# A float32 attention and gated-unit kernel: token sums, weight splits, a query-and-key unit and two steps' loads at other places in the order

## The chip, the cores and the metric

One core of a Trainium2 chip runs the whole program in one launch. The metric is device time in microseconds. The run without a profile was timed three times; the execution that the profile shows is one more run with a time of its own.

## What is computed

The reference, cut to what matters (S=2048 tokens, D=512, H=32 heads of 16, F=1792, float32):

```python
g = sigmoid((x * gate_w).sum(-1, keepdims=True))
q, k, v = split(x @ wqkv)                      # 32 heads of 16
a = softmax(q @ k.T / 4) @ v                   # per head
a = concat(a) @ wo
h = sigmoid(x @ w_gate) * (x @ w_up)
b = h @ w_down
return g * a + (1 - g) * b
```

## The kernel before

Every float32 product is made of three TensorE matmuls on a value's high part and its low part (`h`, `l`): high times high, high times low, low times high. `split` rounds a value to its high part and subtracts it for the low part.

**Startup.** The tokens come as four column blocks `x0` to `x3` of 512 and are split into `xt0` to `xt3` (ring tag "xt", four buffers). Queries and keys of the first head pairs are made at once and sent through DRAM (`q_d`, `k_d`) into the score operands `QS`, `KS`. Then a loop over t = 2, 4, ..., 14 makes the values `v` of two token tiles each, the "token sums". Each pair of sums runs in two halves of the matmul array: first the rows that are LOW for one and UP for the other, then the reverse. Both halves write one PSUM bank, so between them stands a `turn`: an empty instruction in POOL's own queue that waits for the last matmul of the first half, and for which the second half waits (L213 to L218). Since it is in POOL's queue, it also comes after whatever was put there before it. In between, `first_max` makes the first scores and VectorE their row maxima.

POOL's other work is queued in the list `later`, and `work(n)` takes n jobs from it. Generators put jobs there: `filling` (`next(fill)`) the splits of the next query and key weights (`q1`, `k1`) and later the mixtures of weights; `mixing` (`next(mix)`) pieces of token mixtures `xm`, each a load, an addition where it has one, a rounding and a subtraction. In a token sum the last lines are

```python
if g == LOW:
    turn(*two)
    next(mix)
    work(5)
```

**The periods.** 256 periods k (n = 2k) follow, each by a word list (STEADY; for the last eight LAST): score matmuls and exponentials (t), the next scores' row maxima (m), halves of dense work (d). At a period's end come `turn(run)`, `work(...)` and `values(k)`, the product of probabilities and v (L846). The dense work is a list of units: two direct query-key products, three mixed query-key units, 14 gate and up units of the first two token blocks (each made of seven half products of mixtures `xm` and of weight mixtures `mh`, `ml`), then the same for the other blocks, with the query-key unit `qk3_1` at their head (L461 to L463). Last come two down products made ahead, for the token tiles 13 and 4 (SECOND, AHEAD): `hidden_ahead` reads gate and up rows `ha` back from DRAM, makes hidden values on ScalarE and POOL and stores them (`h_d`); `load_ahead` reads them into `hh`.

The row maxima of a group of 16 score tiles are closed by `close_max`: halves on POOL (`mxs`), a transpose on VectorE (`mt`, L345), then `send` (L351): four small DMAs from `mt` into the score operand `qs`. Two groups are sent in four periods; each is needed when, two periods on, its first scores begin.

**The queues.** Nearly all DMAs are issued by SyncE (SP), in order. The instruction order of TensorE, ScalarE, VectorE and POOL is the order of the code; that of SyncE is chosen by the scheduler. SyncE's DMAs signal on eight semaphores in turn, so that one waits for the one eight before it. `take(n)` issues n loads of the list `parts` (late mixtures, `hh`).

**The last loop** goes over 28 steps `chunks` (a token block and two rows of F): `hidden_load` reads gate and up rows (`gul`, 2 x 512 KB), `hidden` and `hidden_split` make hidden values, L1074 multiplies by w_down. Step 0 and 1 are loaded in the periods, 2 to 4 behind them, and each step loads the one five ahead.

Of the kernel before, what the change touches and what calls it, by code (L numbers as in the profile page):

```python
# [26 lines left out]
P = 128  # L27
KT = D // P
# [27 lines left out]
def gated_mix(ctx, tc, x, xc, xmix, wqk, w_qk, wv, wo, w_gu, w_down, gate_w, out):  # L56
# [177 lines left out]
    xes = ExitStack()  # L234
# [3 lines left out]


# [6 lines left out]
    def split_x(c, raw):  # L246
        xt.append(xp.tile([P, 2, KT, 512], F32R, name=f"xt{c}", tag="xt", bufs=4))
        for k in range(KT):
            split(xt[c][:, 1, k, :], xt[c][:, 0, k, :], raw[:, k, :], act, dve)
# [106 lines left out]
    def mixing(pair, T=(), here=0):  # L356
# [27 lines left out]
        for n, (j, b) in enumerate(pieces):  # L384
# [5 lines left out]
            if j < here and b == 0:  # L390
                T[j] = xp.tile([P, 2, KT, 512], F32R, name=f"xm{pair}_{j}", tag="xt", bufs=4)
# [6 lines left out]
    def mixed(pair, j):  # L398
        t = xp.tile([P, 2, KT, 512], F32R, name=f"xm{pair}_{j}", tag="xt", bufs=4)
# [62 lines left out]
    units += [queries_keys(D // P - 1, 1)]  # L462
    units += [gate_up(1, fp, a) for fp in range(NF // 2) for a in range(2)]  # L463

# [54 lines left out]
    def load_ahead(t, lo, hi):  # L519
        if t not in held:  # L520
            held[t] = xp.tile([P, 2, KT, 512], F32R, name=f"hh{t}", tag="xt", bufs=4).rearrange(
# [19 lines left out]
    def filling():  # L541
# [16 lines left out]
        for j, (n, cp) in enumerate(DIRECT):  # L558
            settle([raw for raw, _, _ in coming])
            ws, nxt = nxt, []  # L560
            for c in range(2):
                for i, w in enumerate(ws):
# [6 lines left out]
                    for _ in range(2 if runs < 3 else 1):  # L569
# [16 lines left out]
        for u, (name, _, store) in enumerate(units):  # L586
# [3 lines left out]
            for q, (j, g) in enumerate(order):  # L590
# [7 lines left out]
                leave(e, run.o)  # L598
# [14 lines left out]
                take(1 if u == both - 1 and late_t and q < 4 else 2)  # L613
# [52 lines left out]
    sp.dma_start(gwb, gate_w.unsqueeze(0).to_broadcast([P, D]))  # L666
    next(fill)
# [41 lines left out]
    for t in range(2, NS, 2):  # L709
        two = [Sum(bankv(), tokens(t + a)) for a in range(2)]  # L710
        for g in (LOW, UP):
# [16 lines left out]
            if g == LOW:  # L728
                turn(*two)
                next(mix)  # L730
                work(5)
# [10 lines left out]
    def hidden_load(c, f):  # L742
# [5 lines left out]
        for a in range(2):  # L748
            sp.dma_start(gu[:, a], gu_d[a, f:f + 2, :, c * 512:(c + 1) * 512].rearrange("f p s -> p f s"))
        return gu  # L750

# [165 lines left out]
    ahead_h = []  # L917
    for k in range(NPER):
# [33 lines left out]
        if n in (456, 458, 460, 462, 464, 466):  # L952
            if n % 4 == 0:
                part_ahead = hidden_ahead((n - 456) // 4, SECOND)
            next(part_ahead)
        if n in (304, 308, 312, 316):
            ahead_h.append(hidden_ahead((n - 304) // 4))
            next(ahead_h[-1])
        if n in (308, 312, 316, 320):
            next(ahead_h[(n - 308) // 4])  # L960
# [14 lines left out]
        if k == EARLY - 2:  # L975
            loaded.extend(hidden_load(*chunks[m]) for m in range(2))
        if NPER - TAIL + 2 <= k < NPER - TAIL + 6:
# [19 lines left out]
    loaded.extend(hidden_load(*chunks[m]) for m in range(2, 5))  # L997
# [19 lines left out]
    def heads_split(u, ot, rb):  # L1017
        oh = lp.tile([P, KT, 256], F32R, name=f"oh{u}", tag="oh", bufs=2)
        ol = lp.tile([P, KT, 256], F32R, name=f"ol{u}", tag="ol", bufs=2)
# [127 lines left out]
```

## Time and profile before

| | us |
|---|---|
| runs without a profile | 1667.78, 1663.26, 1664.01 (median 1664.01) |
| the profiled execution | 1670.4 |
| its span, first to last instruction | 1668.2 |
| VectorE, ScalarE, POOL busy in it | 1429.0, 1341.6, 1156.9 |

The page of the profile cuts the span into 40 equal slices of 41.7 us. A digit is the busy share in tenths (9 is 90% or more); PEclk is the clock that TensorE was granted, in tenths of full speed, and GB/s is what the DMA engines moved:

```profile
PE   9799999999999999999999999999999999999999
POOL 1457698978878877767668798777677789864111
PEclk9899999999999999999999999999999999999999
DMA  9535754344453444232664253434343347458871
```

TensorE's row and its clock each have one 7 or 8, in the second slice (41.7 to 83.4 us), which is the token sums' place. The DMA row is full in the first slice (the tokens' loads) and near its end (the last loop's loads).

### The profile page before, as it was taken

How to read it: one execution, taken by the hardware profiler on the slowest of the kernel's cores; microseconds unless marked ns; L12 is line 12 of the kernel's file. 1: busy time of each engine (PE TensorE's matmuls, PEld its weight loads, DVE VectorE, ACT ScalarE, POOL GpSimd, SP SyncE). 2: the span in 40 equal slices, each digit the busy share in tenths (PEclk: the TensorE clock that was granted, in tenths of full speed). 3: DMA queues.
4: the chain of work that ended last, by engine and by line, in shares of the span. 5: the costliest groups of instructions: out<-in, count | busy, mean ns of one | idle time of the engine just before them, and what ended most of it. 6: DMA issues, size and time to landing. Idle time of an engine off the chain costs nothing.

```text
span 1668.2 us, 44281 instructions
## 1 busy us (share of the span) xinstructions
PE 1646.7 (99%) x16830; PEld 1168.4 (70%) x16830; DVE 1429.0 (86%) x2460; ACT 1341.6 (80%) x2944; POOL 1156.9 (69%) x1334
## 2 busy tenths in 40 slices
PE   9799999999999999999999999999999999999999
PEld 7676666667667666666666666666767766667887
DVE  6689999999999999999989999999999999648645
ACT  4168898898889889889879999999999998875322
POOL 1457698978878877767668798777677789864111
PEclk9899999999999999999999999999999999999999
DMA  9535754344453444232664253434343347458871
GB/s 260 153 113 170 212 165 109 116 128 147 133 161 114 138 128 134 84 110 71 183 185 127 82 144 125 102 96 105 95 106 106 90 128 253 131 187 283 267 257 51
DMA packets 136148, 239.87 MB, mean 144 GB/s; under 512 B 19904, under 2 KB 43456, under 8 KB 132928
## 3 DMA queue, kind: packets, MB, share of 16 engines
q1 hardware_dynamic: 135648, 236.52, 47.8%
q8 instruction: 133, 2.18, 0.6%
q14 instruction: 79, 0.65, 0.1%
q10 hardware_dynamic: 288, 0.52, 0.1%
HBM read 161.22 MB, written 75.24 MB: 142 GB/s over the span
## 4 chain that ended last, share of the span: by engine, by line
PE 94%; DMA 3%; DVE 1%; SPq 1%; POOL 1%; ACT 0%; issue 0%; DVEq 0%; ACTq 0%; POOLq 0%
PE dn L178 30%; PE sm L846 16%; PE st L846 12%; PE sm L321 6%; PE sm L700 5%; PE st L700 4%; PE st L321 4%; PE sm L1074 4%; PE st L145 3%; PE dn L158 3%; PE dn L1074 2%; PE st L1074 2%; PE st L158 1%; PE dn L204 1%; PE sm L145 1%; DMA r<-in_w_gu_dram 1%
## 5 line engine op out<-in xcount | busy, mean ns | idle before, releaser
L323 DVE TENSOR_REDUCE stat<-sm 128x1 f32<-128x512 f32 x1199 | 764.2, 682 | 84.5 <-PE st L700 47.1
L702 ACT ACTIVATE p<-sm 128x512 f32<-128x512 f32 (+1 forms) x1308 | 666.6, 598 | 11.4 <-PE sm L700 10.9
L323 DVE TENSOR_REDUCE stat<-st 128x1 f32<-128x512 f32 x849 | 550.4, 683 | 48.1 <-PE sm L700 44.3
L702 ACT ACTIVATE p<-st 128x512 f32<-128x512 f32 (+2 forms) x988 | 519.9, 598 | 0.7
L178 PE MATMUL dn<-xm,mh 64*128 64x512 f32 x1568 | 485.1, 389 | 0.0
L321 PE MATMUL sm<-ks,qs 48*128 48x512 f32 x1199 | 477.2, 420 | 0.5 <-DVE stat L323 0.3
L700 PE MATMUL sm<-qs,ks 64*128 64x512 f32 (+1 forms) x1308 | 471.8, 383 | 4.5 <-DMA qs<-mt 4.5
L700 PE MATMUL st<-qs,ks 64*128 64x512 f32 (+2 forms) x988 | 365.2, 383 | 0.0
L321 PE MATMUL st<-ks,qs 48*128 48x512 f32 x849 | 357.8, 422 | 0.0
L178 PE MATMUL dn<-xm,ml 64*128 64x512 f32 x784 | 304.3, 388 | 0.0
L178 PEld LDWEIGHTS dn<-xm,mh 64*128 64x128 f32 x1568 | 289.9, 185 | 16.1
L846 PE MATMUL sm<-p,v 128*17 128x256 f32 x4704 | 282.5, 381 | 0.0
L700 PEld LDWEIGHTS sm<-qs,ks 64*128 64x128 f32 x1308 | 234.6, 187 | 67.4 <-DVE stat L323 57.5
L321 PEld LDWEIGHTS sm<-ks,qs 48*128 48x128 f32 x1199 | 211.4, 185 | 35.1 <-ACT p L702 26.7
L846 PEld LDWEIGHTS sm<-p,v 128*17 128x17 f32 x4704 | 123.6, 97 | 131.4 <-ACT p L702 44.7
L700 PEld LDWEIGHTS st<-qs,ks 64*128 64x128 f32 x988 | 179.1, 187 | 48.9 <-DVE stat L323 44.5
L846 PE MATMUL st<-p,v 128*17 128x256 f32 x3488 | 209.4, 381 | 0.1
L470 POOL TENSOR_TENSOR m<-m,m 128x512 f32<-128x512 f32 x140 | 178.1, 1289 | 1.3 <-ACT m L630 1.3
L321 PEld LDWEIGHTS st<-ks,qs 48*128 48x128 f32 x849 | 157.5, 185 | 23.5 <-ACT p L702 19.9
L872 POOL TENSOR_TENSOR sum<-sum,part 128x256 f32<-128x256 f32 x192 | 142.0, 739 | 42.2 <-ACT part L851 28.2
L846 PEld LDWEIGHTS st<-p,v 128*17 128x17 f32 x3488 | 91.7, 97 | 97.1 <-ACT p L702 33.2
L178 PEld LDWEIGHTS dn<-xm,ml 64*128 64x128 f32 x784 | 144.4, 184 | 10.6
(381 smaller groups left out, 2473.7 us busy)
## 6 DMA issues: line engine op xcount, KB each, us to landing
r<-in_w_gu_dram SPq DMA_DIRECT2D x112, 256.0 KB
gul<-gu_d SPq DMA_DIRECT2D x56, 512.0 KB
gu_d<-m SPq DMA_DIRECT2D x84, 256.0 KB
xm<-in_xmix_dram SPq DMA_DIRECT2D x24, 512.0 KB
xm_d<-xm SPq DMA_DIRECT2D x24, 512.0 KB
xm<-xm_d SPq DMA_DIRECT2D x24, 512.0 KB
qs<-q_d SPq DMA_DIRECT2D x90, 128.0 KB
ks<-k_d SPq DMA_DIRECT2D x90, 128.0 KB
```

The source lines that it names most:

```text
L145: pe.matmul(o, a, b, start=(i == 0), stop=(i == len(ops) - 1))
L158: mm = pe.matmul(self.o, a[rows], b[rows], start=(self.n == 0), stop=(self.n == 2 * len(self.ops) - 1))
L178: pe.matmul(self.o, a, b, start=(self.n == 0), stop=(self.n == len(self.ops) - 1))
L204: mm = pe.matmul(o, a[rows], b[rows], start=(alone not in self.begun), stop=last)
L321: pe.matmul(t, qs[r:r + KM, qt * P:(qt + 1) * P], ks[r:r + KM, g * 512:(g + 1) * 512], start=True, stop=True)
L323: dve.tensor_reduce(stat[part][:, qt % 4, g:g + 1], t, axis=AX.X, op=ALU.max)
L470: pool.tensor_tensor(o, x, y, op)
L700: pe.matmul(o, ks[r:r + KR, (kt + a) * P:(kt + a + 1) * P], qs[r:r + KR, c * 512 + lo:c * 512 + hi], start=True, stop=True)
L702: exps.append(act.activation(pt[:, a, lo:hi], o, AF.Exp, scale=DH ** -0.5))
L846: pe.matmul(o[r:r + VW, :], v[:, 4 * k % 16 + a, h * VW:(h + 1) * VW], pts[b][:, a, 256 * i:256 * i + 256], start=(a == 0), stop=(a == 3))
L872: added.append(pool.tensor_tensor(s, s, e, ALU.add))
L1074: pe.matmul(down[t], a, b, start=(f == begin and m == 0), stop=(f == NF - 2 and m == 5))
```

## The change

- **Token sums.** `next(mix)` is called once ahead of `next(fill)`, so the first mixture's load is the list's first job and the four weight splits come after it. In the loop over t, `next(mix)` and `work(n)` follow small tables: 1 job at t=2, 4 at t=6, 10 and 12, 12 at t=14, none at 4 and 8. The direct units call `next(mix)` twice after units 1, 3 and 5, where it was after 1 and 2.
- **Buffers.** `tokens_tile` gives the tiles of token block or mixture 3 a buffer of their own (`xq`) and leaves three to the ring of the others. After the last use of mixture 3 its buffer becomes `apart`, which holds the gate and up rows of steps 2 and 3. Behind the periods the steps 4 and 5 are loaded, and each step loads the one six ahead. `oh`, `ol` of the heads move to the side that `xq` frees at step 3.
- **Unit `qk3_1`** stands behind two gate and up units of the second half, no longer ahead of them.
- **Hidden values ahead** for tile 4 are made from n=282 to 310, one part of them at a time (before 304 to 320, overlapping); those for tile 13 from n=448 to 466 (before 456 to 466). The loads of `hh` in the last unit each wait for that unit step's eviction (`left`). In the first unit `take` issues one load, not two, at a time.

```diff
--- before.py
+++ after.py
@@ -231,11 +231,17 @@
     va = keep.tile([P, NS * VROW], F32, name="v", tag="va")
     v = va.rearrange("p (t c) -> p t c", t=NS)
     QS, KS = zip(*[(big(f"qs{b}", F32R), big(f"ks{b}", F32R)) for b in range(2)])
-    xes = ExitStack()
+    xes, xqs = ExitStack(), ExitStack()
+    xq = xqs.enter_context(tc.tile_pool(name="xq", bufs=1, side="right"))
     xp = xes.enter_context(tc.tile_pool(name="xp", bufs=1))
     xt = []
     gwb = xp.tile([P, D], F32, name="gwb")
 
+
+    def tokens_tile(j, name, dt=F32R):
+        if j < 3:
+            return xp.tile([P, 2, KT, 512], dt, name=name, tag="xt", bufs=3)
+        return xq.tile([P, 2, KT, 512], dt, name=name, tag="xt")
 
     def load_x(c):
         raw = mid(f"x{c}")
@@ -244,7 +250,7 @@
         return raw
 
     def split_x(c, raw):
-        xt.append(xp.tile([P, 2, KT, 512], F32R, name=f"xt{c}", tag="xt", bufs=4))
+        xt.append(tokens_tile(c, f"xt{c}"))
         for k in range(KT):
             split(xt[c][:, 1, k, :], xt[c][:, 0, k, :], raw[:, k, :], act, dve)
 
@@ -388,7 +394,7 @@
                 if sign:
                     later.append(lambda n=n, r=rows, op=ALU.add if sign == "+" else ALU.subtract: add(loaded[n], r, op))
             if j < here and b == 0:
-                T[j] = xp.tile([P, 2, KT, 512], F32R, name=f"xm{pair}_{j}", tag="xt", bufs=4)
+                T[j] = tokens_tile(j, f"xm{pair}_{j}")
             later.append(lambda n=n, j=j, b=b: high(loaded[n], j, b))
             later.append(lambda n=n, j=j, b=b: low(loaded[n], j, b))
             if n + 1 < len(pieces):
@@ -396,7 +402,7 @@
         yield
 
     def mixed(pair, j):
-        t = xp.tile([P, 2, KT, 512], F32R, name=f"xm{pair}_{j}", tag="xt", bufs=4)
+        t = tokens_tile(j, f"xm{pair}_{j}")
         for b in range(4):
             parts.append(lambda b=b: sp.dma_start(t[:, :, b, :].bitcast(F32), xm_d[pair, j, :, :, b, :]))
         return t
@@ -459,8 +465,8 @@
     units = [queries_keys(n, 0) for n in range(1, D // P)]
     units += [gate_up(0, fp, a) for fp in range(NF // 2) for a in range(2)]
     both = len(units)
-    units += [queries_keys(D // P - 1, 1)]
     units += [gate_up(1, fp, a) for fp in range(NF // 2) for a in range(2)]
+    units.insert(both + 2, queries_keys(D // P - 1, 1))
 
     def combine(store):
         e = {}
@@ -518,7 +524,7 @@
 
     def load_ahead(t, lo, hi):
         if t not in held:
-            held[t] = xp.tile([P, 2, KT, 512], F32R, name=f"hh{t}", tag="xt", bufs=4).rearrange(
+            held[t] = tokens_tile(0, f"hh{t}").rearrange(
                 "p i k s -> p i (k s)")[:, :, :NF * P].rearrange("p i (f s) -> p i f s", s=P)
         for i in range(2):
             parts.append(lambda i=i: sp.dma_start(held[t][:, i, lo:hi].bitcast(F32), h_d[t][:, i, lo:hi]))
@@ -566,7 +572,7 @@
                     e = keep.tile([P, 512], F32R, name=f"qk{n}_{cp}_{c}_{i}", tag="er", bufs=6)
                     left = leave(e.bitcast(F32), run.o)
                     put_qk(e, (q_d, k_d)[i], n, 2 * cp + c)
-                    for _ in range(2 if runs < 3 else 1):
+                    for _ in range(2 if runs in (1, 3, 5) else 1):
                         next(mix, None)
                     if j + 1 < len(DIRECT):
                         if (c, i) == (0, 0):
@@ -595,7 +601,7 @@
                 yield run
                 m = ((2, 1), (4, 3), (7, 6), (5, 5))[j][g]
                 e = keep.tile([P, 512], F32, name=f"m{m}_{name}", tag="er", bufs=6)
-                leave(e, run.o)
+                left = leave(e, run.o)
                 if arrived:
                     arrived.pop(0)()
                 arrived.append(lambda arrive=arrive, m=m, e=e: arrive(m, e))
@@ -610,7 +616,7 @@
                 last = u == len(units) - 1
                 if last and q in AHEADS:
                     load_ahead(*AHEADS[q])
-                take(1 if u == both - 1 and late_t and q < 4 else 2)
+                take(1 if u == 0 or u == both - 1 and late_t and q < 4 else 2, left if last else None)
                 if last and q:
                     weights_ahead()
             flip ^= 1
@@ -664,6 +670,7 @@
         if c % 2:
             list(load_pair(0, slice((c - 1) * 512, (c + 1) * 512)))
     sp.dma_start(gwb, gate_w.unsqueeze(0).to_broadcast([P, D]))
+    next(mix)
     next(fill)
     w_v = [(wv_h[:, k, :], wv_l[:, k, :]) for k in range(KT)]
     bankv = turns([bankd()] + banks)
@@ -727,8 +734,9 @@
                     closed.append([4, turned])
             if g == LOW:
                 turn(*two)
-                next(mix)
-                work(5)
+                for _ in range({4: 1, 10: 1, 12: 1, 14: 2}.get(t, 0)):
+                    next(mix)
+                work({2: 1, 6: 4, 10: 4, 12: 4, 14: 12}.get(t, 0))
         if t < NS - 2:
             for a in range(2):
                 put_v(t + a, two[a].o, act)
@@ -746,8 +754,11 @@
             gu = big(f"gul{c}_{f}")
         gu = gu.rearrange("p (a f s) -> p a f s", a=2, f=2)
         for a in range(2):
-            sp.dma_start(gu[:, a], gu_d[a, f:f + 2, :, c * 512:(c + 1) * 512].rearrange("f p s -> p f s"))
+            hidden_part(gu, a, c, f)
         return gu
+
+    def hidden_part(gu, a, c, f):
+        sp.dma_start(gu[:, a], gu_d[a, f:f + 2, :, c * 512:(c + 1) * 512].rearrange("f p s -> p f s"))
 
     def late_raw(src, r):
         raw = keep.tile([P, 2, D], F32, name=f"late{r}", tag="ev", bufs=2)
@@ -914,7 +925,6 @@
         put_v(NS - 2 + a, two[a].o, engine)
     bank = bankm = place
     stages = [[], []]
-    ahead_h = []
     for k in range(NPER):
         n = 2 * k
         if 320 <= n < 448 and n % 16 == 0:
@@ -949,15 +959,14 @@
         if k >= EARLY - 4:
             for _ in range((1, 2, 2, 2, 2, 2, 1, 1, 2, 2, 2, 1, 1)[k - EARLY + 4] if k < EARLY + 9 else 0):
                 weights_ahead()
-        if n in (456, 458, 460, 462, 464, 466):
-            if n % 4 == 0:
-                part_ahead = hidden_ahead((n - 456) // 4, SECOND)
+        if n in (448, 452, 454, 458, 462, 466):
+            if n in (448, 454, 462):
+                part_ahead = hidden_ahead((n - 448) // 6, SECOND)
             next(part_ahead)
-        if n in (304, 308, 312, 316):
-            ahead_h.append(hidden_ahead((n - 304) // 4))
-            next(ahead_h[-1])
-        if n in (308, 312, 316, 320):
-            next(ahead_h[(n - 308) // 4])
+        if 282 <= n < 314 and n % 4 == 2:
+            if n % 8 == 2:
+                ahead_h = hidden_ahead((n - 282) // 8)
+            next(ahead_h)
         work(run.jobs if isinstance(run, Side) else 5 if k < 16 or EARLY - 4 <= k < NPER - TAIL else 3 if k % 2 else 4)
         urgent.extend(jobs)
         if 320 <= n < 448:
@@ -974,6 +983,11 @@
         values(k)
         if k == EARLY - 2:
             loaded.extend(hidden_load(*chunks[m]) for m in range(2))
+            apart = tokens_tile(3, "apart", F32)
+            loaded.extend(apart[:, m].rearrange("p (a f) s -> p a f s", a=2) for m in range(2))
+        if EARLY <= k < EARLY + 4:
+            m, a = divmod(k - EARLY, 2)
+            hidden_part(loaded[2 + m], a, *chunks[2 + m])
         if NPER - TAIL + 2 <= k < NPER - TAIL + 6:
             early_hidden(*divmod(k - NPER + TAIL - 2, 2))
         if n == NSTEP - 16:
@@ -994,7 +1008,7 @@
 
     xes.close()
     lp = ctx.enter_context(tc.tile_pool(name="lp", bufs=1))
-    loaded.extend(hidden_load(*chunks[m]) for m in range(2, 5))
+    loaded.extend(hidden_load(*chunks[m]) for m in range(4, 6))
     wd_h = lp.tile([P, NF - 6, D], F32R, name="wd_h")
     wd_l = lp.tile([P, NF - 6, D], F32R, name="wd_l")
     weights = keep.tile([P, NS * VROW], F32R, name="weights", tag="va")
...
@@ -1055,6 +1069,9 @@
     at = dict(zip((9, 11, 13, 15, 18, 20, 23, 25), range(8)))
     heads = {}
     for n, (c, f) in enumerate(chunks):
+        if n == 3:
+            xqs.close()
+            lq = ctx.enter_context(tc.tile_pool(name="lq", bufs=1, side="right"))
         if f == 0:
             down = [bankt() if 4 * c + t != AHEAD else None for t in range(4)] if c else six[2:]
         if n == 4:
@@ -1080,8 +1097,8 @@
                 finish(4 * c + t, o, g0)
             if n == t == 0:
                 last_values()
-        if n + 5 < len(chunks):
-            loaded.append(hidden_load(*chunks[n + 5]))
+        if n + 6 < len(chunks):
+            loaded.append(hidden_load(*chunks[n + 6]))
         if n == 9:
             next(denominators(1))
         if n == 20:
```

What moves on the engines is shown at three places. The names: `q1r`, `k1r` are raw weights and `q1h`, `q1l`, `k1h`, `k1l` their parts; `xm_a_b` is piece b of mixture a; `mtP_i_b` are the maxima of head pair P, query block i, head b; `hN_d` and `haN` are hidden values ahead for tile N; `gu_d` holds gate and up rows; `wdNr` are raw rows of w_down.

**POOL in the token sums.** Rows from the end of the weight splits on (`turn`s are no rows here: before, that of t=4 stands right behind `k1l`; now that of t=6 stands ahead of `q1h` and that of t=8 behind `k1l`). Before:

```order
L131 TENSOR_TENSOR k1l_371<-k1r_366,k1h_370 128x512
L367 TENSOR_TENSOR xm0_0_0_441<-xm0_0_0_441 64x512
L371 CAST xm0_0_520<-xm0_0_0_441 128x512
L376 TENSOR_TENSOR xm0_0_520<-xm0_0_0_441,xm0_0_520 128x512
L367 TENSOR_TENSOR xm0_0_1_524<-xm0_0_1_524 64x512
L371 CAST xm0_0_520<-xm0_0_1_524 128x512
L376 TENSOR_TENSOR xm0_0_520<-xm0_0_1_524,xm0_0_520 128x512
L367 TENSOR_TENSOR xm0_0_2_600<-xm0_0_2_600 64x512
L371 CAST xm0_0_520<-xm0_0_2_600 128x512
L376 TENSOR_TENSOR xm0_0_520<-xm0_0_2_600,xm0_0_520 128x512
L108 CAST mxs_112<-mxs_112 128x4
L109 TENSOR_TENSOR mxs_112<-mxs_112 128x4
```

Now:

```order
L131 TENSOR_TENSOR k1l_374<-k1r_369,k1h_373 128x512
L108 CAST mxs_115<-mxs_115 128x4
L109 TENSOR_TENSOR mxs_115<-mxs_115 128x4
L108 CAST mxs_115<-mxs_115 128x4
L109 TENSOR_TENSOR mxs_115<-mxs_115 128x4
L373 TENSOR_TENSOR xm0_0_0_440<-xm0_0_0_440 64x512
L377 CAST xm0_0_519<-xm0_0_0_440 128x512
L382 TENSOR_TENSOR xm0_0_519<-xm0_0_0_440,xm0_0_519 128x512
L373 TENSOR_TENSOR xm0_0_1_758<-xm0_0_1_758 64x512
```

The halves of the first two maxima (128x4) have moved from behind three pieces of mixture 0 to right behind the weight splits.

**SyncE ahead of the send for period 160** (`mt10_0_0`). Before:

```order
L509 DMA h4_d_79<-ha4_0_13535 256x1x512
L451 DMA gu_d_76<-den_100 128x512
L502 DMA ha4_2_13869<-gu_d_76 128x4x128 x2
L351 DMA qs0_103<-mt10_0_1_13771 2x4x32 x4
L874 DMA pv_d_77<-sum9_2_13557 128x256
L451 DMA gu_d_76<-m3_1_0_1_13529 128x512
L451 DMA gu_d_76<-m1_1_0_1_13373 128x512
L419 DMA r2_1_1_1_14206<-in_w_gu_dram 128x512
L419 DMA r3_1_1_1_14372<-in_w_gu_dram 128x512
L509 DMA h4_d_79<-ha4_1_13696 256x1x512
L502 DMA ha4_3_14034<-gu_d_76 128x2x128 x2
L351 DMA qs0_103<-mt10_0_0_13946 2x4x32 x4
```

Now:

```order
L357 DMA qs1_105<-mt9_3_0_13619 2x4x32 x4
L357 DMA qs0_103<-mt10_0_1_13782 2x4x32 x4
L885 DMA pv_d_77<-sum9_2_13568 128x256
L515 DMA h4_d_79<-ha4_3_13628 256x1x256
L835 DMA xn2_14814<-in_x_dram 128x2x512
L281 DMA k_d_74<-qh3_3_13793 128x512
L281 DMA k_d_74<-den_100 128x512
L425 DMA r2_1_1_1_14214<-in_w_gu_dram 128x512
L357 DMA qs0_103<-mt10_0_0_13954 2x4x32 x4
```

The store and load of `ha4` right ahead of the send are gone; one such store stands five rows ahead, with a logit load behind it, and the stores of the keys of `qk3_1` have come in.

**SyncE around the sends for periods 240 and 244** (`mt15_0_0`, `mt15_1_0`). Before:

```order
L524 DMA hh4_20443<-h4_d_79 128x640 x4
L524 DMA hh4_20443<-h4_d_79 128x512 x2
L351 DMA qs1_105<-mt15_0_0_20522 2x4x32 x4
L113 DMA wd8r_20864<-in_w_down_dram 128x512
L113 DMA wd9r_20868<-in_w_down_dram 128x512
L451 DMA gu_d_76<-den_100 128x512
L749 DMA gul0_0_20979<-gu_d_76 128x2x512 x2
L749 DMA gul0_2_20982<-gu_d_76 128x2x512 x2
L351 DMA qs1_105<-mt15_1_1_20690 2x4x32 x4
```

Now, and, in the second piece, the rows up to the send for period 244:

```order
L530 DMA hh4_20447<-h4_d_79 128x640 x2
L530 DMA hh13_20276<-h13_d_80 128x512 x2
L357 DMA qs1_105<-mt15_0_0_20526 2x4x32 x4
L113 DMA wd8r_20867<-in_w_down_dram 128x512
L113 DMA wd9r_20871<-in_w_down_dram 128x512
L530 DMA hh4_20447<-h4_d_79 128x640 x2
L457 DMA gu_d_76<-den_100 128x512
L113 DMA wd10r_20954<-in_w_down_dram 128x512
L761 DMA gul0_0_20982<-gu_d_76 128x2x512 x2
L761 DMA gul0_2_20985<-gu_d_76 128x2x512
L530 DMA hh4_20447<-h4_d_79 128x512 x2
L357 DMA qs1_105<-mt15_1_1_20694 2x4x32 x4
```

```order
L761 DMA gul0_2_20985<-gu_d_76 128x2x512
L761 DMA apart_20988<-gu_d_76 128x2x512 x2
L457 DMA gu_d_76<-m3_1_6_1_20445 128x512
L457 DMA gu_d_76<-m1_1_6_1_20274 128x512
L113 DMA wd11r_20958<-in_w_down_dram 128x512
L761 DMA apart_20988<-gu_d_76 128x2x512 x2
L113 DMA wd4r_21044<-in_w_down_dram 128x512
L357 DMA qs1_105<-mt15_1_0_20861 2x4x32 x4
```

The six loads of `hh4` in one go ahead of the first send have become three pairs, two of them behind it; four loads into `apart` (512 KB each) are new ahead of the second.

More of the change, by code (lines that the diff above doesn't have):

```diff
@@ L1017, in heads_split @@
     def heads_split(u, ot, rb):
-        oh = lp.tile([P, KT, 256], F32R, name=f"oh{u}", tag="oh", bufs=2)
-        ol = lp.tile([P, KT, 256], F32R, name=f"ol{u}", tag="ol", bufs=2)
+        oh = lq.tile([P, KT, 256], F32R, name=f"oh{u}", tag="oh", bufs=2)
+        ol = lq.tile([P, KT, 256], F32R, name=f"ol{u}", tag="ol", bufs=2)
         for j in range(2):
```

## The prediction

> **What bounds the kernel now.** The page comes first: busy time by engine, then the chain that ended last.
>
> ```profile
> PE 1646.7 (99%) x16830; PEld 1168.4 (70%) x16830; DVE 1429.0 (86%) x2460; ACT 1341.6 (80%) x2944; POOL 1156.9 (69%) x1334
> ```
>
> ```profile
> PE 94%; DMA 3%; DVE 1%; SPq 1%; POOL 1%; ACT 0%; issue 0%; DVEq 0%; ACTq 0%; POOLq 0%
> ```
>
> TensorE is busy 99% of the span of 1668.2 us and carries 94% of the chain. The change takes no matmul away, so what it can gain is TensorE's idle time and the time at a reduced clock. The view of TensorE's waits lists nearly all of the first:
>
> ```profile
> PE dn L158 <- POOLq L215: 10.0, 1, 10.0
> PE sm L700 <- DMA qs<-mt: 4.5, 3, 2.7
> PE sm L1074 <- DVE hl L109: 1.4, 1, 1.4
> ```
>
> Five waits, then: one at the start (a turn, L215), three in the periods (row maxima that come late from `send`, L351), one in the last loop. Each is followed to its cause.
>
> **The startup wait.** TensorE's timeline (start, length, engine, line, tiles; in brackets the idle time before it and what ended it):
>
> ```profile
> 44.49 0.50 PE L321 MATMUL sm<-ks,qs 48*128 48x512 f32 x2
> 54.97 0.79 PE L158 MATMUL dn<-wv_h,xt 64*128 64x512 f32 x1 [9.97 <-POOLq L215]
> ...
> 58.87 0.39 PE L158 MATMUL dn<-wv_h,xt 64*128 64x512 f32 x1
> 59.10 0.39 PE L158 MATMUL dn<-wv_h,xt 64*128 64x512 f32 x1
> ```
>
> Pairs of half-array matmuls start 0.23 us apart (58.87, 59.10). Between the lower halves of the token sums t=4 and their upper halves lie 54.97 - 44.49 = 10.48, so 10.25 are lost. From 54.97 to 58.87 the order has nine places (eight pairs of halves and a pair of scores), which take 3.90 instead of 9 x 0.23 = 2.07: another 1.83. The windows view shows the clock of that stretch:
>
> ```profile
> 55.00:59.60 4.60, 4.60 (x26) 3.64 (x28) 1.24 (x2) 0.00 (x0) 4.37 (x4) 0.59 0.29 48
> ```
>
> The last three numbers are the granted clock (0.59), the share of the DMA engines and GB/s. The cause is on POOL's timeline:
>
> ```profile
> 52.36 0.61 POOL L135 CAST q1h<-q1r 128x512 fp32r<-128x512 f32 x1 [43.54 <-DMA q1r<-in_wqk_dram]
> ...
> 54.94 1.27 POOL L131 TENSOR_TENSOR k1l<-k1r,k1h 128x512 fp32r<-128x512 f32 x1
> ...
> 72.72 1.29 POOL L376 TENSOR_TENSOR xm<-xm,xm 128x512 fp32r<-128x512 f32 x1
> 73.97 0.18 POOL L108 CAST mxs<-mxs 128x4 fp32r<-128x4 f32 x1
> ```
>
> `work(5)` at t=2 puts the four splits of q1 and k1 into POOL's queue, the first waits until 52.36 for its weights, and the turn of t=4 stands behind k1l (54.94). In the change t=2 pops only the first mixture's load and the splits come behind the turn of t=6. Turn t=4 then meets an empty queue: **-10.25, and -1.83** for the clock that fell with it. Late next is the turn of t=8, behind k1l, which still ends at 54.94 + 1.27 = 56.21. The sums of t=8 begin at 66.74 now (next part), so 12.1 earlier at 54.7, and their upper half half of 6.9 later, at 58.1: 1.9 us of cover. What the weights land later than that is lost.
>
> **Token sums t=10.** The scores' first call marks where a pair of sums begins (t=8, 10, 12, 14, then the first period); the row apart is VectorE's:
>
> ```profile
> 66.74 0.40 PE L321 MATMUL sm<-ks,qs 48*128 48x512 f32 x2
> 73.64 0.46 PE L321 MATMUL sm<-ks,qs 48*128 48x512 f32 x2
> 82.55 0.49 PE L321 MATMUL sm<-ks,qs 48*128 48x512 f32 x2
> 89.56 0.40 PE L321 MATMUL sm<-ks,qs 48*128 48x512 f32 x2
> ...
> 98.40 0.39 PE L321 MATMUL sm<-ks,qs 48*128 48x512 f32 x1
> ```
>
> ```profile
> 74.47 0.31 DVE L345 STREAM_TRANSPOSE mt<-mxs 128x128 f32<-128x128 f32 x1 [1.88 <-POOL mxs L109]
> ```
>
> t=8 takes 6.90, t=10 **8.91**, t=12 7.01: 1.96 over the mean of its neighbours. VectorE stood 1.88 before the transpose because the maxima's halves (73.97) were queued behind a mixture piece (72.72 and its two neighbours); TensorE then ran out of score banks. In the change the halves stand right behind k1l, ahead of any piece, on an idle POOL. Bounds: all of 1.96 goes, or only 1.0 (the halves still take two small operations and a hop each way). I take **-1.6**, near the full amount, since the piece in front is gone altogether.
>
> The pieces land elsewhere: twelve jobs at t=14 are three pieces, each (1.29 + 0.61 + 1.29, some 3.3 with gaps), 10 us of POOL from about 79.0 (89.56 + 3.4 - 14), ending near 89 or, with the maxima's halves between them, 89.5. The first turn of the periods is queued behind them and needed when the second period begins, 98.40 - 14 + 5.4 = 89.8: nothing in the best case, 3.0 if the last piece's load is a piece (3.3) late. I take **+0.4**, near the lower end, as the queue alone just fits.
>
> **The three late maxima.** SyncE's timeline (its DMA issues) ahead of each, and the transpose that made the data ready, for the two whose queue changes:
>
> ```profile
> 965.67 0.59 SPq L509 DMA_DIRECT2D h_d<-ha  x1
> 968.72 0.89 SPq L502 DMA_DIRECT2D ha<-gu_d  x2
> 969.70 2.67 SPq L351 DMA_DIRECT2D qs<-mt  x4
> ...
> 1399.90 2.76 SPq L524 DMA_DIRECT2D hh<-h_d  x6
> 1402.75 2.65 SPq L351 DMA_DIRECT2D qs<-mt  x4
> ```
>
> ```profile
> 961.68 0.30 DVE L345 STREAM_TRANSPOSE mt<-mxs 128x128 f32<-128x128 f32 x1
> ```
>
> At 961.98 the maxima were ready; the queue held them 7.7 us, first for POOL's hidden-ahead values, then for the loads behind that store. TensorE lost about 0.9, so a send may start some 6.8 late before it costs anything. In the change the hidden-ahead work comes five to eleven periods earlier, one part at a time, so POOL is not behind when this store comes: **-0.9**. The third stands behind six hh loads in one burst; in the change two are taken per unit step, each behind its eviction, and part-ahead starts four periods earlier: **-0.9** (4.5 - 2.7 leaves 1.8 for both). Bounds for the pair: 0 to -1.8.
>
> The first and largest is different:
>
> ```profile
> 850.70 1.23 SPq L401 DMA_DIRECT2D xm<-xm_d  x2
> 851.99 2.57 SPq L419 DMA_DIRECT2D r<-in_w_gu_dram  x4
> 854.66 3.82 SPq L351 DMA_DIRECT2D qs<-mt  x4
> ```
>
> ```profile
> 851.33 1.06 PE L846 MATMUL st<-p,v 128*17 128x256 f32 x16
> 856.76 1.27 PE L846 MATMUL st<-p,v 128*17 128x256 f32 x20
> 867.67 1.92 PE L846 MATMUL sm<-p,v 128*17 128x256 f32 x32
> ```
>
> ```profile
> 861.30:864.60 3.30, 3.23 (x17) 2.78 (x19) 2.05 (x3) 2.16 (x5) 0.04 (x1) 0.50 0.68 235
> ```
>
> The values of a period come every 5.43 (851.33, 856.76), here after 10.91: 5.48 lost, the wait of 2.7 and a half clock (0.50) after it. Ahead of the send stand the late mixtures' loads and the raw rows of one unit. The change replaces a query-and-key unit's raw rows there by a gate-and-up unit's, of the same sizes in the same order; the mixtures' loads stay. So **0**; bound -5.5.
>
> **Tail and the two steps loaded early.** The 1.4 before L1074 belongs to the fifth step, whose eviction waits for rows that come last in a crowded queue. In the change they keep their place, behind five other loads of 512 KB: **0**, bound -1.6 (the wait with its restart). Four such loads more, written for periods 244 to 247, stand in SyncE's order close ahead of the send for period 244, 2.1 MB. What flows there now, in five microseconds each:
>
> ```profile
> 1405.00:1410.00 5.00, 4.12 (x53) 2.42 (x51) 3.76 (x9) 3.64 (x9) 4.92 (x8) 1.00 0.81 267
> 1415.00:1420.00 5.00, 5.00 (x60) 3.39 (x57) 4.72 (x11) 4.04 (x10) 4.84 (x6) 1.00 0.97 359
> ```
>
> Over two periods (10.9 us) they add 193 GB/s to 267, and 460 is 101 above the 359 that were carried: 1.1 MB, or 3.1 us behind. They use an empty buffer and nothing waits for them; a send behind them may. I take **0**, as 3.1 is under the cover of 6.8; bounds 0 and +5.5, the price of the period above. The moved unit's stores and the logit loads have work around them on every engine; a missed place costs a period's tenth at most: 0.
>
> **Sum.** -10.25 - 1.83 - 1.6 + 0.4 - 0.9 - 0.9 = -15.1. Of the profiled execution's own 1670.4 us (span 1668.2) 1655.3 would be left. The runs without a profile have a median of 1664.0 (1663.3 to 1667.8), 6.4 less; the terms are stalls of the program's order and not of the profiler, so I take them off that: **1648.9, say 1649**.
>
> **Rivals.**
> 1. *The stall at period 140 goes as well*, since its cause is lateness of transfers, and a shifted POOL or fewer takes in the first unit may empty the queue. For it: the send needs to gain only some 3 us. Against: rows and order ahead of it are the same. 1649 - 5.5 = 1643.5, with the tail's 1.6 gone 1642.
> 2. *A new late send at period 244*, behind the added loads: +0.9 (like 160) to +5.5 (like 140), so 1650 to 1654.5. For it: 460 GB/s has no room, and the send is right behind. Against: 3.1 of the 6.8 is used.
> 3. *The startup wait only moves to t=8* (the change doesn't do what it says), if the weights of q1 and k1 land over 1.9 later; each further microsecond costs one. Twelve late would give 10.1 back: 1659. Against: their loads keep their place in the queue.
> 4. *Slower*: SyncE's queue falls behind from 240 to 255 for good, because each hh load waits for an eviction and holds all that is behind it, while the added loads fill the transfers. All four lower sends of that stretch would then stall like period 140: 4 x 5.5 = 22, or 1671. It decides where sends start more than 6.8 late four times running; above 20.1 added the kernel is slower by over 0.3%. Now only one of these four is late, by 0.9.
>
> The trace has a wait of 2.7 us followed by a clock of 0.50. The Trainium skill ("TensorE: Matmul & The Clock Gate", What's actually happening) has the gate throttle after at least one idle window of about 3.4 us, free-running, and open again after as much work. By that a wait of 2.7 would cost 2.7 alone, rival 2 would end at 1651.7, and rival 4 would come to 4 x 2.7 - 15.1, still faster. The trace disagrees on the length (2.7 was enough) and agrees on the way back (3.9 us at half speed after the first wait).
>
> **How the numbers follow.** Forecast 0.53 (its own range 1646 to 1652), rival 1 0.22, rival 2 0.17, rival 3 0.05, rival 4 0.03. The range runs from rival 1 with the tail (1642) to rival 2's end with the first turn's bound (1654.5 + 2.6, about 1657); 8 in 100 lie outside. A measurement of this kernel tells 0.3% (5 us) from no change: faster 0.92 (forecast, rivals 1 and 2), same 0.05 (rival 3), slower 0.03.
>
> **What will show it.** The row of L215 at 10 us gone from TensorE's waits; token sums t=4 and t=10 at 6.9 to 7.0 like the others; no clock under 0.9 between 40 and 80; k1l's end at about 56 and the turn of t=8 without idle time. Waits for qs<-mt: one of about 2.7 near 845, and nothing near 959 and 1393; a row near 1414 is rival 2. The forecast is wrong if startup still has a wait over 2 us, or if more than one send is late behind the periods' middle.

## The result, and the profile after

| | us |
|---|---|
| before, without a profile | 1664.13 (median of 6, 1663.26 to 1667.78) |
| changed, without a profile | 1655.76 (median of 6, 1654.81 to 1658.87) |
| ratio | 0.9948, 95% interval 0.9935 to 0.9961 |
| profiled execution, before and changed | 1670.4 and 1655.2 (spans 1668.2 and 1653.0) |

Faster by about 8.4 us, inside the stated range, but 6.8 above the forecast of 1649. The two profiled executions differ by 15.2 us, almost exactly the 15.1 of the forecast's sum. That agreement is an accident, as the sections below show: most of the sum's terms were right, three costs were missing, and the first profile of the kernel before held a stall that is much smaller in every other one.

TensorE's waits in the changed kernel, in the form shown for before (released by, total us, times, longest):

```profile
PE sm L707 <- DMA qs<-mt: 2.9, 2, 1.7
PE st L93 <- DVE warm L89: 1.0, 1, 1.0
PE dn L158 <- POOLq L215: 0.5, 1, 0.5
```

The turn's wait of 10.0 in the startup is gone; the 0.5 belongs to another turn, one of a direct query-key product. The late maxima come to 2.9 in two waits (4.5 in three), and the last loop's 1.4 is gone. Apart from the 1.0 ahead of the warm-up matmuls, none of these waits is where one was before. POOL's timeline of the changed token sums:

```profile
53.40 0.61 POOL L135 CAST q1h<-q1r 128x512 fp32r<-128x512 f32 x1 [44.58 <-DMA q1r<-in_wqk_dram]
...
56.02 1.29 POOL L131 TENSOR_TENSOR k1l<-k1r,k1h 128x512 fp32r<-128x512 f32 x1
61.50 0.19 POOL L108 CAST mxs<-mxs 128x4 fp32r<-128x4 f32 x1 [4.19 <-DVE mxs L341]
...
67.29 1.29 POOL L373 TENSOR_TENSOR xm<-xm 64x512 f32<-64x512 f32 x1 [3.19 <-DMA qs<-mt]
```

The weights still land late (53.40), but no turn waits for them now, and the maxima's halves (61.50) find POOL idle. The calls that mark the starts of t=8, 10 and 12, and of the first period:

```profile
55.59 0.40 PE L327 MATMUL sm<-ks,qs 48*128 48x512 f32 x2
...
62.51 0.45 PE L327 MATMUL sm<-ks,qs 48*128 48x512 f32 x2
...
70.07 0.53 PE L327 MATMUL sm<-ks,qs 48*128 48x512 f32 x2
...
85.96 0.39 PE L327 MATMUL sm<-ks,qs 48*128 48x512 f32 x1
```

The first period starts at 85.96 (98.40 before): 12.4 earlier, though this execution began later by itself. The 16 warm-up matmuls at the very start, the same in both kernels, before and changed:

```profile
1.02 5.26 PE L93 MATMUL st<-warm 128*128 128x512 f32 x16 [1.02 <-DVE warm L89]
```

```profile
1.02 6.25 PE L93 MATMUL st<-warm 128*128 128x512 f32 x16 [1.02 <-DVE warm L89]
```

They end 1.0 us later here, and some 0.8 of it is left at the upper half of t=4 (its first call at 45.32, before at 44.49). So token sums and turn have gained about 13.3 (12.4 and 0.8).

What is new is a late send at period 16. A period's length is taken here from the start of its values to the start of the next period's; undisturbed it is 5.43.

```profile
171.95 0.84 PE L857 MATMUL sm<-p,v 128*17 128x256 f32 x12
...
175.60 0.32 PE L707 MATMUL sm<-qs,ks 64*128 64x192 f32 x1 [1.73 <-DMA qs<-mt]
...
180.61 0.62 PE L857 MATMUL st<-p,v 128*17 128x256 f32 x8
```

```profile
175.00:180.00 5.00, 4.40 (x27) 3.56 (x29) 3.27 (x5) 3.62 (x8) 4.84 (x8) 0.68 0.56 134
```

Period 15's values at 171.95 are followed by the next after 8.66 instead of 5.43: 1.73 of waiting and a clock of 0.68 behind it cost 3.23. SyncE's timeline shows what stands ahead of the send:

```profile
164.89 0.34 SPq L368 DMA_DIRECT2D xm<-in_xmix_dram  x1
165.33 1.25 SPq L407 DMA_DIRECT2D xm<-xm_d  x2
166.66 0.54 SPq L281 DMA_DIRECT2D q_d<-qh  x1
167.30 0.39 SPq L281 DMA_DIRECT2D q_d<-qk  x1
167.78 0.66 SPq L385 DMA_DIRECT2D xm_d<-xm  x1
168.54 3.13 SPq L357 DMA_DIRECT2D qs<-mt  x4
```

and the chain ahead of the wait:

```profile
165.33 5.70 DMA xm<-xm_d
171.05 4.42 DMA qs<-mt
```

One piece of a token mixture is loaded and another stored ahead of the send, with two 512 KB loads of the late mixtures between them; the send's fourth DMA waits for one of those loads (5.70) and lands after 4.42 itself. The send starts 2.0 us into its period (168.54, the period's values at 166.52); in the kernel before, the same send started 0.7 into it. The rows ahead of it were the same there, in the same order, but earlier in their period: the piece's load waits until its buffer's store has landed, and that store now starts 1.0 us later and takes 8.1 to land (6.1 before), so that the load goes out 1.6 us ahead of the values instead of 4.7.

Two smaller ones: a turn of the direct products costs 0.7 at period 9 (period 8 lasts 6.16; a mixture piece stands ahead of the turn in POOL's queue until 135.9), and a send for period 244 costs 1.2, rival 2's place. That send's second DMA goes out at 1410.93, when a load into `apart` that was issued eight DMAs before it, at 1402.23, has landed. Periods 160 and 240 are clean, as forecast.

### The profile page after: what moved, and what is told of

Its sections match the earlier page's. It is cut to its first block, busy times and chain, and to the rows that moved or that the text cites. A ratio compares the mean times of both kernels' runs of the same rounds, so it can differ in the third digit from the quotient of the medians.

```text
span 1653.0 us, 44265 instructions
## 1 busy us (share of the span) xinstructions
PE 1644.4 (99%) x16830; PEld 1168.0 (71%) x16830; DVE 1428.8 (86%) x2460; ACT 1341.1 (81%) x2944; POOL 1158.5 (70%) x1334
## 4 chain that ended last, share of the span: by engine, by line
PE 95%; DMA 2%; POOL 1%; ACT 1%; DVE 0%; issue 0%; SPq 0%; POOLq 0%; ACTq 0%
PE dn L178 31%; PE sm L857 16%; PE st L857 12%; PE sm L327 6%; PE sm L707 5%; PE sm L1091 4%; PE st L707 4%; PE st L327 4%; PE st L145 3%; PE st L1091 2%; PE dn L158 2%; PE dn L1091 2%; PE st L158 1%; PE sm L145 1%; ACT p L709 1%; DMA gu_d<-m 1%
```

## The experiments

Each ratio is to runs of the kernel before that were made beside it, so experiments are compared by their ratios; the brackets hold its 95% interval.

**The kernel before, profiled again** (no edit).

> The kernel before, unchanged, profiled a second time. Question: is the 5.5 us stall of period 140 part of every execution? Theory A (it is one execution's, set off by late transfers): TensorE's waits for qs<-mt have no row near 2.7, the period with values at 856.76 takes about 5.4 like the others, and the span is 1661 to 1663.5. Theory B (it belongs to the program's order, and the change took it away): it is there again with 2 to 3 us of waiting, span 1666 to 1669. By both, the turn's wait of 10 us (L215) and two waits of about 0.9 at periods 160 and 240 are there.

One run, 1665.37, span 1663.1. TensorE's waits:

```profile
PE dn L158 <- POOLq L215: 11.2, 1, 11.2
PE sm L700 <- DMA qs<-mt: 2.0, 2, 1.1
PE st L93 <- DVE warm L89: 1.0, 1, 1.0
PE sm L1074 <- DVE hl L109: 0.7, 1, 0.7
```

No wait near 2.7, and the span is theory A's. Period 139 lasts 6.59 here (10.91 in the first profile), not 5.4; it has one of the two waits that are left, and the other is that of period 160. Period 240 has none, which neither theory had. The start is again a turn of over 10 us. So the 5.5 us of period 140 were one execution's, on top of a send that is close to its limit (in the changed kernel's two profiles that period lasts 5.51 and 6.91). The difference is most of the first profile's 6.4 us over the median.

**The token-sum edits alone**, on before:

```diff
+    next(mix)
     next(fill)
...
-                next(mix)
-                work(5)
+                for _ in range({4: 1, 10: 1, 12: 1, 14: 2}.get(t, 0)):
+                    next(mix)
+                work({2: 1, 6: 4, 10: 4, 12: 4, 14: 12}.get(t, 0))
...
-                    for _ in range(2 if runs < 3 else 1):
+                    for _ in range(2 if runs in (1, 3, 5) else 1):
```

> Before, with only the token-sum edits of the change: one call of the mixture generator ahead of the weight splits, the two tables over t, and the direct units' calls after units 1, 3 and 5. Theory A (the changed kernel's new waits at periods 9 and 16 come from the mixture pieces that these edits move later): startup 13.3 us shorter, the turn's wait of about 0.5 near 135 and a late send near 173 are there, cost 0.7 + 3.2, so 9 to 10 us less than before: about 1654.5; the two waits of 0.9 stay. Theory B (those waits come from the three-buffer ring or from the other edits): neither wait is there, 13.3 less: about 1651.

1653.52, ratio 0.9942 (0.9927 to 0.9957): theory A. The turn's 0.5 is there, period 8 lasts 6.14 and period 15 lasts 8.17, as in the changed kernel:

```profile
PE sm L701 <- DMA qs<-mt: 4.5, 3, 2.7
PE st L93 <- DVE warm L89: 1.0, 1, 1.0
PE dn L158 <- POOLq L215: 0.5, 1, 0.5
```

The 2.7 is now period 16's; 0.9 each stay at 160 and 240. These edits alone bring the whole gain of the change (its ratio of 0.9948 lies in their interval).

**The token-sum edits with one piece more in startup**, on before. The pieces keep the old kernel's pace in the direct units:

```diff
-                next(mix)
-                work(5)
+                for _ in range({4: 1, 10: 2, 12: 1, 14: 2}.get(t, 0)):
+                    next(mix)
+                work({2: 1, 6: 4, 10: 8, 12: 4, 14: 12}.get(t, 0))
```

> Before, with the token-sum edits but two mixture pieces behind the turn of t=10 (one more piece done in startup) and the direct units' calls after units 1 and 2 as before. Theory A (pace of the pieces): the row of 10 us is gone, there is no wait of a turn near 135 and none over 0.5 us for a late send near 173, so about 13 less than before: 1651. Theory B (the two waits come from elsewhere): they stay, and it takes about what the startup edits alone take. Both: the two pieces end by about 74, as the turn of t=12 is needed, so up to 0.5 of waiting there.

1653.44, ratio 0.9938 (0.9923 to 0.9953). No wait at 9 and none at 16, as theory A has it, but the time is that of the startup edits alone, as theory B has it. A turn's wait of 1.0 in the first periods takes part of the gain back: the sixth piece's load comes behind eight small DMAs of a send, and POOL waits 2.64 for it ahead of the turn. Another 1.1 is a wait in the last loop, which nothing here explains.

**The change without its token-sum edits** (their lines as in before).

> The changed kernel with the token-sum edits undone (buffers, unit, loads ahead and hidden values stay changed). Theory A (terms add up): the turn's wait of 10 us and its slow clock are back, the two waits of 0.9 at periods 160 and 240 are gone, the late send at period 244 costs about 1.2, no waits at 9 and 16: 0.3 to 1 us less than before, about 1663.4. Theory B (the other edits bring part of the 8.4 us): 3 to 5 us less than before, about 1660.

1664.27, ratio 1.0004 (0.9994 to 1.0014): theory A's 0.3 to 1 us less lies within the interval. The turn's wait is back (9.6), 160 and 240 are clean, 244 costs 1.2. All other parts of the change together are worth nothing that can be measured.

**The loads into apart two periods later**, on the changed kernel:

```diff
-        if EARLY <= k < EARLY + 4:
-            m, a = divmod(k - EARLY, 2)
-            hidden_part(loaded[2 + m], a, *chunks[2 + m])
+        if EARLY + 2 <= k < EARLY + 6:
+            m, a = divmod(k - EARLY - 2, 2)
+            load = hidden_part(loaded[2 + m], a, *chunks[2 + m])
+            tc.add_manual_dep(load.ins, lately[0].ins.name, SYNC, reason="not ahead of the maxima")
```

> The changed kernel with one difference: the four loads into apart are issued two periods later and each behind an exponential of its period (246 to 249), so that they stand behind the sends for periods 244 and 248. Theory A (the new wait near 1414 comes from these 2.1 MB ahead of the send): no wait for qs<-mt near 1414, steps 2 and 3 are there in time, 1.2 us less than the changed kernel: 1654.6. Theory B (the hidden loads of hh, each behind an eviction, hold the queue): the wait stays at about 1.2, 1655.8.

1654.08, ratio 0.9937 (0.9922 to 0.9952). The wait at 244 is gone, in favour of theory A; the time alone couldn't tell it. SyncE's order up to period 16 is the changed kernel's, and yet period 15 lasts 6.86 here: the wait at 16 is there again, at less than half its price.

**The earlier piece, on the changed kernel** (two pieces behind the turns of t=10 and t=14, the rest of the table as above with `14: 8`, direct units as in before).

> The changed kernel with two mixture pieces behind the turn of t=10 and two behind that of t=14, and the direct units' calls after units 1 and 2: one piece is done earlier. Theory A (the waits at periods 9 and 16 come from pieces that run late beside the late mixtures' loads): both waits gone, nothing over 0.3 at the first periods' turn, 3.5 us less than the changed kernel: 1652. Theory B (the wait at 16 comes from the late mixtures' own loads, which stay): the turn's 0.5 goes, 1 to 3 us at period 16 stay: 1654.5 to 1655.

1652.59, ratio 0.9923 (0.9908 to 0.9937). The turn's 0.5 is gone and period 15 lasts 6.58 (8.66 in the changed kernel, but 6.86 in the experiment just above). So the pace of the pieces makes the turn's wait, theory A; at 16 1.1 is left, as theory B has it, and how much the pace is worth there doesn't follow from this pair. The table at the end of this section answers it.

**Both.**

> Both edits on the changed kernel: the earlier piece and the later loads into apart. If the terms add up, TensorE's waits hold nothing but the first 1.0 of the warm-up and less than 1 us in the periods: 4.7 us less than the changed kernel, 1651, with a span of 1648.5 to 1649.5. If one of the two repairs only moves its wait: 1653 to 1655.

1654.65, ratio 0.9930 (0.9915 to 0.9945): not 1651, but the range named for a repair that only moves its wait. The waits at 9 and 244 are gone, but waits of 1.3 at period 140 and 0.9 at 16 stay, period 32 lasts 0.6 longer, and a wait of 1.3 is back in the last loop. SyncE's order up to period 16 is now that of the next kernel, and the send starts at the same place in its period (0.7). The next kernel has no wait there, so what is left at 16 is transfer time, not order.

**The token-sum edits with the earlier piece, on before** (the third experiment with `14: 8`).

> Before with the token-sum edits and the earlier piece only (two pieces behind the turns of t=10 and t=14), with none of the other edits. Startup 13.3 us shorter, no wait of the first periods' turn (1.0 with three pieces behind t=14), no waits at periods 9 and 16, the two waits of 0.9 at periods 160 and 240 stay. Theory A (the other edits are worth those two waits, 1.8): 1652, about 1 over the changed kernel with both repairs. Theory B (they are worth nothing, since the waits they remove come and go): the same as that kernel within 0.5.

1650.80, ratio **0.9911** (0.9897 to 0.9925): faster than the changed kernel, whose interval lies wholly above this one. TensorE's waits (at 140 and 160; 240 has none) and SyncE's rows ahead of period 16:

```profile
PE sm L701 <- DMA qs<-mt: 1.2, 2, 0.9
PE st L93 <- DVE warm L89: 1.0, 1, 1.0
```

```profile
159.77 0.34 SPq L362 DMA_DIRECT2D xm<-in_xmix_dram  x1
160.76 1.24 SPq L401 DMA_DIRECT2D xm<-xm_d  x2
162.09 0.54 SPq L275 DMA_DIRECT2D q_d<-qh  x1
162.81 0.33 SPq L275 DMA_DIRECT2D q_d<-qk  x1
164.74 0.58 SPq L379 DMA_DIRECT2D xm_d<-xm  x1
165.41 2.76 SPq L351 DMA_DIRECT2D qs<-mt  x4
```

The piece's load now comes 5.6 ahead of the send (3.7 in the changed kernel): its buffer's store lands after 5.8 here and after 8.1 there. Neither theory had a time this low. Against the changed kernel with the earlier piece (0.9908 to 0.9937) the lead isn't clear of noise, so whether the other parts cost something was still open; they were added to this kernel one by one.

**Only the hidden values' new times and the single hh loads** on top.

> The startup edits with the earlier piece (the fastest kernel so far, 1650.8, ratio to before 0.9911) and, of the change's other parts, only the hidden values ahead at their new times and the loads of hh each behind an eviction. Theory A (the waits of 0.9 at periods 160 and 240 are all that this part moves): both gone, nothing new, ratio 0.990 to 0.991. Theory B (single loads behind evictions hold SyncE's queue): a wait for qs<-mt between periods 236 and 248, ratio 0.992 or more.

1649.58, ratio 0.9912 (0.9900 to 0.9925). The wait of 0.9 at period 160 is gone (240 had none in the kernel without this part):

```profile
PE st L701 <- DMA qs<-mt: 1.4, 1, 1.4
PE st L93 <- DVE warm L89: 1.0, 1, 1.0
PE sm L1074 <- DVE hl L109: 0.2, 1, 0.2
```

but one of 1.4 has come at period 152, where loads of the hidden values ahead now stand ahead of a send. No other profile with these times has it. There is no gain that can be measured, and no loss either.

**Only the moved unit and the first unit's single takes** on top.

> The startup edits with the earlier piece and, of the other parts, only the moved unit qk3_1 and the single takes of the first unit. Theory A (this part costs nothing): waits of 0.9 near periods 160 and 240 as before, ratio 0.991. Theory B (it is what makes the changed kernel slower than the startup edits): new or longer waits between periods 16 and 32 or 136 and 180, ratio 0.993.

1659.59, ratio 0.9967 (0.9955 to 0.9980): 9 us lost, theory B.

```profile
PE dn L178 <- ACT m L630: 5.3, 1, 5.3
PE sm L701 <- DMA qs<-mt: 1.3, 1, 1.3
```

```profile
960.59 0.60 ACT L630 ACTIVATE m<-dn 128x512 f32<-128x512 f32 x1 [6.15 <-DMA q_d<-m_qk]
```

With the old times of the hidden values, the unit's stores and the hidden values meet: an eviction waits 6.15 for the buffer of a store that is stuck in SyncE's queue, behind loads of hidden values that wait until a store of such values has landed (issued at 951.31, landed at 954.32). TensorE waits for the eviction, and period 159 lasts 13.57. In the changed kernel, which has both the move and the earlier hidden values, that period lasts 5.43: the move needs them.

**Only the buffers** on top.

> The startup edits with the earlier piece and, of the other parts, only the buffers: three in the ring, one apart, steps 2 and 3 loaded early, each step loading the one six ahead. Theory A (the loads into apart collide with a send): a wait for qs<-mt of 1 to 2.7 near period 244, no wait in the last loop, ratio 0.992 to 0.993. Theory B (they cost nothing): no wait there, ratio 0.991.

1655.34, ratio 0.9943 (0.9930 to 0.9957): theory A for the place, and more than its price.

```profile
PE sm L707 <- DMA qs<-mt: 4.8, 4, 1.6
```

1.5 of it lies at 244, where the loads into apart stand ahead of the send:

```profile
1399.75 2.92 SPq L761 DMA_DIRECT2D apart<-gu_d  x3
...
1405.33 0.87 SPq L761 DMA_DIRECT2D apart<-gu_d  x1
1406.29 0.76 SPq L113 DMA_DIRECT2D wd4r<-in_w_down_dram  x1
1407.15 4.83 SPq L357 DMA_DIRECT2D qs<-mt  x4
```

The other three are at 140, 160 and 240. The one at 160 is that of the kernel without this part (6.36 against 6.33); the other two are longer than there (7.02 and 6.26, against 5.78 and 5.54), and the last loop has a wait of 0.7, where theory A had none. Of what this part costs only the 1.5 is traced to it. Why 140 and 240 are longer isn't settled: they lie before the first load into apart, and kernels without it have shown 6.75 and 6.32 there.

**The changed kernel again** (no edit).

> The changed kernel, unchanged, on the same chip as the three others and with a second profile. Theory A (its waits belong to its order): the turn's 0.5 at period 9 and a wait at period 16 of 1 to 3 us with a late send (two microseconds later in its period than before) are there again, and one at period 244; ratio 0.994 to 0.996. Theory B (they were one execution's): two of the three are gone, and the time falls in with the startup edits alone, ratio under 0.993.

1656.09, ratio 0.9950 (0.9938 to 0.9963), theory A: periods 8, 15 and 243 last 6.16, 8.87 and 6.12 (6.16, 8.66 and 6.65 in the first profile). These waits belong to the order.

**All fourteen profiles side by side.** They answer what single pairs leave open. "Old" and "new" are the lines of the kernel before and of the change; the four with the new token-sum tables are the changed kernel's two, the token-sum edits alone and the loads into apart two periods later:

| period | profiles | its length, us |
|---|---|---|
| 8 | 4 with the new token-sum tables | 6.14 to 6.16 |
| 8 | 10 with the old ones or the earlier piece | 5.43 |
| 15 | 4 with the new token-sum tables | 6.86 to 8.87 |
| 15 | 10 with the old ones or the earlier piece | 5.43 in eight, 6.35 and 6.58 in two |
| 159 | 7 with the old times of the hidden values | 6.32 to 6.36, and 13.57 with the moved unit |
| 159 | 7 with the new times | 5.43 |
| 239 | 7 with the old times | 6.26 to 6.32 in three, 5.43 to 5.67 in four |
| 239 | 7 with the new times | 5.43 |
| 243 | 5 with the loads into apart in their new place | 6.12 to 6.94 |
| 243 | 9 without them or with later ones | 5.43 |
| 139 | all | 10.91 once, 5.43 to 7.02 in the others |

The send for period 16 starts 1.7 to 2.9 us into its period in the four profiles and 0.7 in the ten; the four have one and the same order of SyncE up to there, and one of them has no other part of the change, so the late send comes from the token-sum tables. The two of the ten with a wait are the changed kernel with the earlier piece; whether the other parts have a hand in that last 1 us isn't shown. In all five profiles with a wait at 244 the send's second DMA waits for a load into `apart` that was issued eight DMAs before it.

## Why the prediction was right and where it failed

- *Startup wait and clock, -12.1, and t=10, -1.6:* right in mechanism and size. About 13.3 was gained in all; t=10 gave 1.35 of it (it lasts 7.56), and the first turn's +0.4 did not occur. The cover for the turn of t=8 was enough, so rival 3 is out.
- *Periods 160 and 240, -1.8:* right for the changed kernel. The wait at 160 is in six of the seven profiles with the old times (the seventh, with the moved unit, has a longer stall there) and in none with the new ones. That at 240 is in three of seven with the old times, so the second 0.9 isn't there every time.
- *Period 140, 0:* the argument (same rows, same order) was right, the price was not: 5.5 was one execution's value of a wait that costs 0 to 1.6 in the other thirteen profiles. The wait of about 2.7 near 845 that should have stayed isn't there. Rival 1 "came true" only between the two first profiles.
- *What the pieces' new places cost:* the step that failed. It followed the pieces to the end of startup and stopped there. One piece fewer in startup means one more among the direct units, beside the late mixtures' loads, and this costs 0.7 at period 9 and 1.4 to 3.4 at period 16 (3.2 and 3.4 in the changed kernel). The token-sum edits alone show both costs; the earlier piece takes the first away, and of the second leaves nothing or about 1. The cover should have been read at each send, not once: 6.8 us at period 160, but nearly none at 16. There the kernel before starts its send 0.7 into the period, and two kernels with that very start have waits of 1.1 and 0.9.
- *Loads into apart, 0:* rival 2 happened at the low end, 0.7 to 1.2 in the changed kernel. The prediction set 3.1 us of backlog in bytes against the 6.8 of cover. What held the send was the queue: its second DMA had to wait until a load into `apart`, issued eight DMAs before it, had landed.
- *The moved unit, 0:* right only together with the earlier hidden values; alone it costs 9.

With these, -13.3 + 0.7 + 3.2 + 1.2 - 1.8 = -10.0, against -8.4 measured (the interval is -10.8 to -6.5). These are one profile's sizes, and the 1.6 between the two isn't traced to a place. That the time lies inside the range is in part luck: the upper end stood for rival 2 and a late first turn, which came to 1.2 and to nothing, and the 3.9 of the pieces took that room. Rival 4, the slower one, had no part in it: behind period 240 only the send for 244 is late, by 0.7 to 1.2.

## What to carry to other kernels

An empty instruction that serves as a fence in an engine's queue waits for what is queued ahead of it there: look at what those neighbours wait for. When work moves out of a crowded place, follow it to where it lands and read the slack there, send by send. And take a second profile before a single large stall is priced: of the 5.5 us at period 140, other executions show 0 to 1.6.

## What the runs showed of the hardware

- The same 16 matmuls at the start took 5.26 us in one execution and 6.25 in another (5.20 to 6.61 over all profiles here). Between the first two profiles some 0.8 of that was still there at t=4.
- The turn goes on when the POOL instruction ahead of it starts, not when it ends: `k1l` runs from 54.94 to 56.21, and TensorE goes on at 54.97; in the kernel with one piece more in startup the last subtraction ahead of the turn runs from 93.23 to 94.52, and TensorE goes on at 93.26. The prediction took the end, 56.21, for the turn of t=8, so its cover was larger than it said.
- How a wait affects the clock isn't given by its length. 1.73 us of waiting at period 16 was followed by a clock of 0.68 and cost 3.23; in the token-sum edits alone, 2.7 at the same place left the clock at full speed and cost 2.74:

```profile
175.00:180.00 5.00, 4.29 (x45) 3.23 (x49) 3.75 (x7) 3.93 (x10) 4.84 (x8) 1.00 0.57 132
```

The clock records of the traces show the rest. Between the program's start and its end the half clock comes in stretches of 3.41, 6.83 or 10.24 us (one, two and three times 3.41; 176.83 to 180.24 in the changed kernel), and within an execution their borders lie on one grid of 3.41. What seems to count is how much of a wait falls into one step of that grid: 1.73 and 1.94 us in one step (the changed kernel's two profiles) and 2.19 (period 140 in the first profile of before) were followed by the half clock, 1.58 and less were not. The 2.7 in the token-sum edits alone was split by a border into 1.76 and 0.97 and was not. By these few cases the limit is near half a step; more of them could move it.

The Trainium skill ("TensorE: Matmul & The Clock Gate", What's actually happening) has a free-running window of about 3.4 us, and the grid of 3.41 agrees; that it takes at least one whole idle window doesn't fit the 1.73.
